# Attention and FFN in one kernel: when the rest rows' weights are combined, and how they are stored

## The chip, the cores and the metric

One of the 8 cores of a Trainium2 chip runs the whole kernel. The metric is the device time of one execution in microseconds (us). TensorE (PE) multiplies, VectorE (DVE), ScalarE (ACT) and GpSimd (POOL) work element by element, SyncE (SP) issues nearly all DMAs of this kernel. Each engine works its instructions off in program order.

## The reference

```python
def _A_ref(x, wqkv, wo):                       # B=1, S=2048, D=576
    H = 32; Dh = D // H; W, dil = 8, 2
    q, k, v = ...                              # x @ wqkv, per head
    idx = pos[:, None] - off[None, :]          # off = arange(W) * dil
    logits = einsum("bhsd,bhswd->bhsw", q, kg) * Dh ** -0.5   # masked where idx < 0
    attn = softmax(logits)
    return einsum("bhsw,bhswd->bhsd", attn, vg) ... @ wo
def _B_ref(x, w1, b1, w2):                     # F = 4608
    h = x @ w1 + b1
    act = h * tanh(softplus(h))                # Mish
    return act @ w2
xn = _layernorm(x)
return x + _A_ref(xn, A_wqkv, A_wo) + _B_ref(xn, B_w1, B_b1, B_w2)
```

Attention looks at 8 earlier tokens, two apart. All tensors are float32.

## The kernel before, in words

**Tiling.** The 2048 tokens are worked in two halves (hf 0 and 1) of 1024, each in two blocks of 512. Every float32 operand of a matmul is split into a high part (a cast to fp32r, ScalarE) and a low part (a subtraction, VectorE), and a product is three matmuls. QKV and the first FFN matmul (w1) are computed as a Strassen-like scheme of 7 products (B11, B21, B22, T3, T1, T2, T4) over 4 of the 4.5 tiles of 128 that make up D = 576. The sums of activations that it needs are S0 to S3 (`s_step`, GpSimd; `s_high`, ScalarE; `s_low`, VectorE). The last 64 rows of D, two blocks of 32, are the rest: their products, high and low rows side by side on the 128 partitions, need only one matmul for each of the 7 (`xt,wr`, `rest_y,xt` in the profile).

**Stages.** First layer norm, transposes and the first units of QKV (steps "q": PE lines 361, 363, 670, 676), which I call the prologue. Then QKV's second half by the 7 products (steps "y", line 791). Then 18 quads of the FFN for half 0, each of six parts of w1 (line 1100) with pairs of the w2 matmul (line 1197) between them, and attention's element work on GpSimd and VectorE underneath. Then the transition: QKV of half 1 (steps "v" and "z"), and the quads of half 1, which use what half 0 kept in DRAM (`kept_...`). The output projection comes last.

**Chunks.** The rest rows of the weights have to be combined (four subtractions give the other combinations from four blocks) and split as well. This is done for chunks: 0 to 3 (128 rows for four quads of w1 each), 4 (64 rows, two quads), and y and v (QKV). A chunk goes through five functions, one plan step apart: `c_load` (SyncE, line 869), `c_sum` (4 subtractions on GpSimd, line 874), `c_high` (cast on ScalarE, line 877), `c_low` (subtraction on VectorE, line 881) and `c_keep` (2 stores to the DRAM tiles `ckept`, line 889). Later `wr_fetch` (line 896) loads the 7 x 128 rest weights of a quad into one of the two buffers "wc", and `rest_fetch` (line 905) those of y, v and z. Before the change all seven chunks are made in the prologue. ck_4 has the buffer of ck_v and can be loaded when ck_v has been stored.

**What sets the order.** The program first makes a list `plan` of steps, each with foreground and background functions, filled by `put`, `before` and a table `MOVED`; then it runs the list, and each engine has its instructions in the order in which they were written. `spot(hf, q, i)` is slot i of quad q. A DMA that SyncE issues also waits for the one eight earlier on its lane, since there are eight semaphore lanes.

**Other names.** `rest_dup` copies the rest rows four times side by side before the transposes; `rest_split` splits what the transposes give; `qkv_send` stores finished rows of k, v and q in DRAM (`kv_d`, `q_d`, lines 691 and 696), from which attention reads them (lines 916 and 925).

## Time and profile before

| | |
|---|---|
| median of 3 runs | 1179.85 us (1179.37 to 1182.48) |
| profiled execution, its time | 1179.86 us |
| its span, first to last instruction | 1177.8 us |
| mean granted clock of TensorE | 0.971 |
| busy share PE, PEld, DVE, ACT, POOL | 93%, 85%, 77%, 45%, 68% |
| HBM read and written | 180.51 MB and 115.38 MB |

PEld is TensorE's weight load, which goes on beside the matmuls. In the rows of slices, the span is cut in 40 and a digit is the busy share in tenths; PEclk is the granted clock in tenths of full speed. A row of waits reads: engine and line that waited, the tile it needed, what made it last, then us in total, times, and the longest. In a row of the timeline the square bracket holds the idle time before it and what ended that. In a row of the chain stand start, us, engine or DMA and what it worked on.

### The profile page before, as it was taken

The page shows a single profiled execution, that of the slowest core. Times are in us where ns is not written, and L with a number is a line of the kernel's source. Part 1 is how long each engine was busy: PE and PEld are TensorE (multiplying, and loading weights), DVE is VectorE, ACT ScalarE, POOL GpSimd, SP SyncE. Part 2 cuts the span into 40 slices and gives each one's busy share as a digit, 9 for nine tenths or more (in the row PEclk, how much of TensorE's full clock was granted, in tenths as well). Part 3 has the DMA queues.
Part 4 walks back from the last instruction along what each step waited for, and adds up shares of the span by engine and source line. Part 5 has one row for each costly group of instructions (what it writes and reads, how often), then busy time and mean ns, then how long its engine had stood idle before and what let it go on. Part 6 is the DMA issues. An engine that isn't in the chain of part 4 may idle for free.

```text
span 1177.8 us, 18410 instructions
## 1 busy us (share of the span) xinstructions
PE 1094.1 (93%) x6414; PEld 999.1 (85%) x6414; DVE 911.9 (77%) x1505; ACT 525.0 (45%) x975; POOL 800.8 (68%) x649
## 2 busy tenths in 40 slices
PE   8706999999999999999988888999999999999998
PEld 7605989999999999989987767998988998999998
DVE  7608679888989878898786546688788888688886
ACT  7503555455445544445642205444443444244343
POOL 5207549767885777897587546977868688978533
PEclk9857999999999999999999989999999999999999
DMA  7545989988788787977479989988676867679864
GB/s 261 178 141 168 299 288 362 320 279 261 224 295 275 244 260 261 312 245 280 138 257 274 286 254 303 331 279 262 206 247 206 274 197 238 198 257 310 266 209 145
DMA packets 203300, 297.13 MB, mean 252 GB/s; under 512 B 63334, under 2 KB 137608, under 8 KB 203208
## 3 DMA queue, kind: packets, MB, share of 16 engines
q1 hardware_dynamic: 203208, 295.96, 77.9%
q8 instruction: 51, 0.84, 0.3%
q14 instruction: 41, 0.34, 0.1%
HBM read 180.51 MB, written 115.38 MB: 251 GB/s over the span
## 4 chain that ended last, share of the span: by engine, by line
PE 72%; DMA 10%; POOL 6%; DVE 5%; issue 3%; SPq 2%; ACT 2%; POOLq 0%; DVEq 0%; ACTq 0%
PE h L1100 29%; PE po L1197 16%; PE po L1289 10%; PE po L1311 6%; PE o L1476 5%; PE y L791 2%; POOL pv L1000 2%; DMA ckept_v<-ck_v 1%; DMA ckept<-ck 1%; DMA acc<-in_x 1%; POOL pr L961 1%; PE z L791 1%; DMA wr<-ckept 1%; DMA q<-q_d 1%; PE yT L791 1%
## 5 line engine op out<-in xcount | busy, mean ns | idle before, releaser
L1197 PEld LDWEIGHTS po<-w,act 128*128 128x128 f32 x1728 | 236.0, 188 | 7.7 <-DVE acc L1201 2.6
L1197 PE MATMUL po<-w,act 128*128 128x288 f32 x1728 | 241.1, 295 | 1.2 <-DVE acc L1201 1.1
L961 POOL TENSOR_TENSOR pr<-q,kv 128x576 f32<-128x576 f32 x128 | 194.3, 1544 | 26.0 <-DMA q<-q_d 11.8
L1000 POOL TENSOR_TENSOR pv<-L,kv 128x576 f32<-128x576 f32 x128 | 173.3, 1454 | 51.0 <-DVE L L993 13.6
L1150 POOL TENSOR_TENSOR act<-c,act 128x512 fp32r<-128x512 f32 x66 | 90.9, 1377 | 80.5 <-ACT act L1148 74.1
L1289 PEld LDWEIGHTS po<-pw,u 128*128 128x128 f32 x1008 | 137.8, 188 | 6.4 <-issue 2.0
L1289 PE MATMUL po<-pw,u 128*128 128x288 f32 x1008 | 141.1, 295 | 1.5 <-DMA pw<-kept_T 0.8
L1201 DVE TENSOR_TENSOR acc<-po,acc 128x288 f32<-128x288 f32 x288 | 118.8, 448 | 26.5 <-PE po L1197 25.1
L1006 DVE TENSOR_REDUCE og<-pv 128x144 f32<-128x1152 f32 x64 | 86.1, 1347 | 33.1 <-POOL pv L1000 33.1
L1100 PE MATMUL h<-xt,t 128*128 128x512 f32 x432 | 110.9, 391 | 0.7 <-DVE rt L1142 0.5
L1100 PE MATMUL h<-S,t 128*128 128x512 f32 x432 | 110.3, 391 | 0.0
L1100 PE MATMUL h<-xt,wa 128*128 128x512 f32 x432 | 109.8, 389 | 0.0
L1100 PE MATMUL h<-xt,wr 128*128 128x512 f32 x252 | 98.3, 390 | 3.7 <-DMA wr<-ckept 3.7
L1143 ACT ACTIVATE c<-c,cb 128x512 f32<-128x512 f32 x69 | 50.0, 725 | 108.9 <-DVE c L1142 108.8
L966 DVE TENSOR_REDUCE L<-pr 128x64 f32<-128x1152 f32 x64 | 85.5, 1340 | 16.6 <-POOL pr L961 16.4
L1100 PEld LDWEIGHTS h<-xt,wa 128*128 128x128 f32 x432 | 81.0, 188 | 16.5
L1100 PEld LDWEIGHTS h<-xt,t 128*128 128x128 f32 x432 | 78.9, 188 | 16.4 <-DVE rt L1142 1.3
L1100 PEld LDWEIGHTS h<-S,t 128*128 128x128 f32 x432 | 78.0, 188 | 13.2 <-ACT rm L1131 0.4
L670 PE MATMUL pq<-wq,xt 128*128 128x432 f32 x192 | 46.1, 387 | 38.9 <-ACT xt L367 38.0
L1311 PEld LDWEIGHTS po<-w,act 128*128 128x128 f32 x576 | 78.4, 188 | 1.6
L1311 PE MATMUL po<-w,act 128*128 128x288 f32 x576 | 79.5, 294 | 0.0
L1131 ACT COPY c<-h 128x512 f32<-128x512 f32 x68 | 39.8, 585 | 86.6 <-PE h L1100 86.6
(314 smaller groups left out, 2139.4 us busy)
## 6 DMA issues: line engine op xcount, KB each, us to landing
kv<-kv_d SPq DMA_DIRECT2D x64, 396.0 KB
kept_t<-t SPq DMA_DIRECT2D x36, 512.0 KB
t<-kept_t SPq DMA_DIRECT2D x36, 512.0 KB
wr<-ckept SPq DMA_DIRECT2D x72, 224.0 KB
pw<-kept_T SPq DMA_DIRECT2D x24, 576.0 KB
rw<-in_w SPq DMA_DIRECT2D x36, 288.0 KB
kept_B<-w SPq DMA_DIRECT2D x36, 288.0 KB
pw<-kept_B SPq DMA_DIRECT2D x18, 576.0 KB
```

The costliest lines, as they stand in the source:

```text
L961: nc.gpsimd.tensor_tensor(out=pr[:, x:x + hh], in0=q[:, j0 + x:j0 + x + hh, None, :].to_broadcast([P, hh, W, CU]), in1=win(kt, 0, CU, j0 + ...
L966: nc.vector.tensor_reduce(L[:, k, j0:j0 + hj].rearrange("p j w h -> p (j w h)"), pr.rearrange("p j w (h d) -> p (j w h) d", h=2), axis=AX, ...
L1000: nc.gpsimd.tensor_tensor(out=pr[:, x:x + hj].rearrange("p j d w -> p j w d"), in0=L[:, k, x:x + hj, :, h:h + 1].to_broadcast([P, hj, W, DH]),
L1006: nc.vector.tensor_reduce(og[:, c0:c0 + DH, :].rearrange("p d j -> p j d"), pr, axis=AX, op=ALU.add)
L1100: nc.tensor.matmul(ph, l, r_, start=first and i == 0, stop=i == len(seq) - 1, skip_group_check=True)
L1143: nc.scalar.activation(t, ph if fresh else t, AF.Mish, bias=b1c[:, f:f + 1])
L1150: eng.tensor_tensor(out=a[:, 1, :], in0=t, in1=a[:, 0, :].bitcast(F32), op=ALU.subtract)
L1197: nc.tensor.matmul(po, acts[hf, q, b, j][:, al, tok], done["w2", hf, 2 * q + j][:, wl, c * HC:(c + 1) * HC], start=i == 0, stop=i == 5)
L1201: nc.vector.tensor_tensor(out=t, in0=po, in1=t, op=ALU.add)
L1289: nc.tensor.matmul(po, units[e, k, qq][:, al, tok], w[:, qq, wl, :], start=i == 0, stop=i == 5)
L1311: nc.tensor.matmul(po, acts[hf, q, b, j][:, al, tok], done["w2", hf, 2 * q + j][:, wl, c * HC:(c + 1) * HC], start=i == 0, stop=i == 5)
L1476: nc.tensor.matmul(h, l, r_, start=first and n == 0, stop=n == len(seq) - 1, skip_group_check=True)
```

## The change

Only chunk 0 and y are made in the prologue. Chunks 1 to 4 and v are made as ten pieces of half the columns ("10", "11", ..., "41", "v0", "v1"), one in each of the quads 1 to 10 of half 0, in slots 0 (load), 1 (sum), 2 (high), 3 (low) and 4 (stores), in buffers of the tag "wc" that wr has too. wr of the next quad is fetched in slot 6 instead of 2 (q < 12). High and low rows alternate by partition instead of standing in blocks of 32; the DRAM tiles `ckept` have one row for each partition of a chunk, so that chunk 0 and y are stored as 128 rows. `qkv_send` of y, v and z comes a plan step later and in the background list. The last split of `rest_split` is a foreground function of the next step. In half 1 the sums S3 come ahead of S2.

On SyncE in the prologue (rows in program order; the shape behind the names is the access pattern), before, from the stores of ck_305 (chunk 2) on:

```order
L691 DMA kv_d_128<-kvs_0_1_446 128x8x144
L696 DMA q_d_132<-qs_0_1_447 128x4x144
L889 DMA ckept_627<-ck_305 4x32x896 x2
L723 DMA yB_0_633<-in_wq 128x432
L889 DMA ckept_v<-ck_v 4x32x756 x2
L869 DMA ck_4_659<-in_w1r 64x512
L723 DMA yB_0_662<-in_wq 128x432
L723 DMA yB_0_664<-in_wq 128x432
L889 DMA ckept_690<-ck_3_308 4x32x896
L889 DMA ckept_690<-ck_3_307 4x32x896
```

and now, from the stores of ck_301 (chunk 0) on:

```order
L895 DMA ckept_528<-ck_301 128x896 x2
L895 DMA ckept_y<-ck_y 128x756 x2
L596 DMA kept_wq_567<-wq_3_244 128x864
L723 DMA yB_0_569<-in_wq 128x432
L723 DMA yB_1_571<-in_wq 128x432
L691 DMA kv_d_128<-kvs_0_1_431 128x8x144
L696 DMA q_d_132<-qs_0_1_432 128x4x144
L723 DMA yB_0_594<-in_wq 128x432
L723 DMA yB_0_616<-in_wq 128x432
L723 DMA yB_0_618<-in_wq 128x432
L723 DMA yB_1_645<-in_wq 128x432
L723 DMA yB_1_668<-in_wq 128x432
```

The stores of chunks 1, 2, v and 3 and the load of ck_4 no longer stand between the loads of yB; the two chunks left have 128 rows in a store.

On ScalarE at the same place (xn_6 is the tile of tokens that is transposed next), before:

```order
L877 CAST ck_v<-ck_v 128x756
L331 CAST xt_1_569<-ss_0_585 128x4x128
L677 COPY kvs_0_1_446<-pq_0_1_3_608 128x8x36
L678 COPY qs_0_1_447<-pq_0_1_3_608 128x4x36
L877 CAST ck_3_308<-ck_3_307 128x896
L367 CAST xt_1_569<-ta_635 128x4x128
L331 CAST xt_1_569<-tb_636 128x128
L331 CAST a21t<-tb_636 128x128
L478 ACTIVATE xn_6_666<-acc_1_2_188,nm_167,rs_165 128x576
L380 COPY rd_6_668<-xn_6_666 128x256
```

and now:

```order
L677 COPY kvs_0_1_431<-pq_0_1_3_573 128x8x36
L678 COPY qs_0_1_432<-pq_0_1_3_573 128x4x36
L331 CAST xt_1_541<-ss_0_557 128x4x128
L367 CAST xt_1_541<-ta_596 128x4x128
L331 CAST xt_1_541<-tb_597 128x128
L331 CAST a21t<-tb_597 128x128
L478 ACTIVATE xn_6_620<-acc_1_2_188,nm_167,rs_165 128x576
L380 COPY rd_6_622<-xn_6_620 128x256
```

The casts of ck_v and ck_3 are gone, and the cast of xt from ss stands behind the copies of kvs and qs.

On ScalarE in quad 1 of half 0 (ck_1455 is the first piece, half of chunk 1), before:

```order
L1143 ACTIVATE c_0_1_1501<-c_0_1_1501,cb 128x512
L1148 CAST act_0_2_1523<-c_0_1_1501 128x512
L1131 COPY c_0_1_1555<-h_0_1_1493 128x512
L577 CAST w_0_3_1594<-rw_3_1464 128x576
L577 CAST t_0_2_1596<-tt_1514 128x512
L1131 COPY c_0_1_1608<-h_0_1_1493 128x512
L630 CAST twhT_1_1617<-twT_1_1559 128x576
```

and now:

```order
L1150 ACTIVATE c_0_1_1443<-c_0_1_1443,cb 128x512
L1155 CAST act_0_2_1467<-c_0_1_1443 128x512
L1138 COPY c_0_1_1500<-h_0_1_1435 128x512
L883 CAST ck_1455<-ck_1455 128x448
L577 CAST w_0_3_1540<-rw_3_1406 128x576
L577 CAST t_0_2_1542<-tt_1458 128x512
L1138 COPY c_0_1_1555<-h_0_1_1435 128x512
L630 CAST twhT_1_1567<-twT_1_1505 128x576
```

The cast of the piece stands ahead of the casts of w and t and of the second copy of c.

On SyncE in the same quad, before:

```order
L596 DMA kept_wc_1491<-wc_1_1442 128x512
L916 DMA kv_0_2_1541<-kv_d_127 128x792
L925 DMA q_2_1543<-q_d_131 128x288
L896 DMA wr_2_1545<-ckept_503 64x896 x2
L596 DMA kept_t_1_1598<-t_0_1_1462 128x1024
L596 DMA kept_wa_1612<-wa_2_1519 128x1024
L500 DMA rw_5_1614<-in_w 128x576
```

and now:

```order
L903 DMA wr_2_1614<-ckept_528 64x1x896 x2
L596 DMA kept_t_2_1631<-t_0_2_1542 128x1024
L500 DMA rw_4_1633<-in_w 128x576
L500 DMA rw_6_1635<-in_w 128x512
L500 DMA rw_7_1637<-in_w 128x512
L645 DMA kept_T_0_1639<-twhT_1_1567 256x1x288
L646 DMA kept_T_0_1639<-twT_1_1505 256x1x288
L592 DMA kept_B_0_1675<-w_0_2_1453 128x2x288
L592 DMA kept_B_0_1677<-w_0_3_1540 128x2x288 x2
L645 DMA kept_T_0_1683<-twhT_1_1612 256x1x288
L646 DMA kept_T_0_1683<-twT_1_1557 256x1x288
```

The load of the piece follows kept_wc; its two stores follow kept_t, and wr_2 comes behind them and behind kept_wa and rw_5.

On SyncE in the transition, before:

```order
L839 DMA z_B_0_0_6804<-kept_yB_0_941 128x432
L839 DMA z_B_0_1_6805<-kept_yB_0_941 128x432
L691 DMA kv_d_127<-kvs_v_6727 128x8x144
L696 DMA q_d_131<-qs_v_6726 128x4x144
L839 DMA z_B_1_0_6836<-kept_yB_1_968 128x432
L839 DMA z_B_1_1_6837<-kept_yB_1_968 128x432
L905 DMA rest_v_6847<-ckept_v 64x8x108 x2
L916 DMA kv_0_12_6879<-kv_d_130 128x792
```

and now:

```order
L839 DMA z_B_0_0_6847<-kept_yB_0_883 128x432
L839 DMA z_B_0_1_6848<-kept_yB_0_883 128x432
L839 DMA z_B_1_0_6876<-kept_yB_1_910 128x432
L839 DMA z_B_1_1_6877<-kept_yB_1_910 128x432
L912 DMA rest_v_6890<-ckept_v 64x4x216 x2
L691 DMA kv_d_127<-kvs_v_6769 128x8x144
L696 DMA q_d_131<-qs_v_6768 128x4x144
L923 DMA kv_0_12_6924<-kv_d_130 128x792
```

The stores of kvs_v and qs_v moved behind the loads of z_B and rest_v.

The diff, cut to these parts:

```diff
         last_ = []
-        plan[now[0] + 1][1].append(lambda: last_.append(split(X[:, 9:13, at_], ss)))
-        plan[now[0] + 2][1].insert(0, lambda: last_[0]())
+        plan[now[0] + 1][0].append(lambda: last_.append(split(X[:, 9:13, at_], ss)))
+        plan[now[0] + 1][0].append(lambda: last_[0]())
...
-        nc.scalar.copy(t.rearrange("p (k c d) -> p k c d", k=2, c=4), xns[hf, n][:, KT * P:D].rearrange(
-            "p (k d) -> p k d", k=2)[:, :, None, :].to_broadcast([P, 2, 4, RB]))
+        nc.scalar.copy(t.rearrange("p (k c d e) -> p k c d e", k=2, c=2, e=2), xns[hf, n][:, KT * P:D].rearrange(
+            "p (k d) -> p k d", k=2)[:, :, None, :, None].to_broadcast([P, 2, 2, RB, 2]))
...
         if half and jj == JB - 1 and (add_ or name == "B22"):
-            qkv_send(hf, g0 + g, b, kvs, qs)
+            plan[now[0] + 1][1].append(lambda: qkv_send(hf, g0 + g, b, kvs, qs))
...
-    CORDER = ("B11", "B21", "B22", "T3", "T1", "T2", "T4")
+    CORDER = ("B11", "B21", "B22", "T3", "T2", "T1", "T4")
     chunk, ckept, rcols = {}, {}, {}
 
+    def c_tiles(c):
+        return 7, QC if c[0] in "yv" else P, 64 if c[0] == "4" else P
+
     def c_load(c):
-        n, w, rows = (7, QC, P) if c in "yv" else (7, P, P if c != "4" else 64)
-        tag = {"0": "S0", "1": "S1", "2": "S2", "3": "wa", "4": "pr", "y": "kv", "v": "pr"}[c]
-        if tag[0] == "S":
-            t = sb.tile([P, 2, 2 * TB], F32, tag=tag, bufs=1, name=f"ck_{c}")
-            lo, hi = (t[0:rows, k, 0:n * w].rearrange("p (n w) -> p n w", n=n) for k in range(2))
+        n, w, rows = c_tiles(c)
+        cols = slice(0, w)
+        if c == "0":
+            t = sb.tile([P, 2, 2 * TB], F32, tag="S0", bufs=1, name="ck_0")
+            lo, hi = (t[:, k, 0:n * w].rearrange("p (n w) -> p n w", n=n) for k in range(2))
+        elif c == "y":
+            lo, hi = (sb.tile([P, n, w], F32, tag="kv", bufs=3, name=f"ck{k}_y") for k in range(2))
         else:
-            lo, hi = (sb.tile([P, n, w], F32, tag=f"wa{k}" if tag == "wa" else tag, bufs=dict(wa=1, pr=2, kv=3)[tag],
-                              name=f"ck{k}_{c}")[0:rows] for k in range(2))
-        chunk[c] = lo, hi.bitcast(F32R)
-        src = wqr["vy".index(c)] if c in "yv" else w1r[int(c) * P:int(c) * P + rows]
-        nc.sync.dma_start(lo[:, 0:4], src)
+            cols = slice(int(c[1]) * w // 2, (int(c[1]) + 1) * w // 2)
+            t = sb.tile([P, 2, n, w // 2], F32, tag="wc", bufs=2, name=f"ck_{c}")
+            lo, hi = t[0:rows, 0], t[0:rows, 1]
+        chunk[c] = lo, hi.bitcast(F32R), cols
+        src = wqr["vy".index(c[0])] if c[0] in "yv" else w1r[int(c[0]) * P:int(c[0]) * P + rows]
+        nc.sync.dma_start(lo[:, 0:4], src[:, :, cols])
 
     def c_sum(c):
         lo = chunk[c][0]
-        for o, a, b in ((4, 3, 0), (3, 2, 3), (5, 2, 4), (6, 1, 5)):
+        for o, a, b in ((5, 3, 0), (3, 2, 3), (4, 2, 5), (6, 1, 4)):
             nc.gpsimd.tensor_tensor(out=lo[:, o], in0=lo[:, a], in1=lo[:, b], op=ALU.subtract)
 
     def c_high(c):
         nc.scalar.copy(chunk[c][1], chunk[c][0])
 
     def c_low(c):
-        lo, hi = chunk[c]
+        lo, hi, _ = chunk[c]
         nc.vector.tensor_tensor(out=lo.bitcast(F32R), in0=lo, in1=hi.bitcast(F32), op=ALU.subtract)
 
     def c_keep(c):
-        lo, hi = chunk[c]
-        m = lo.shape[0] // RB
-        ckept[c] = dram.tile([2, RB, CP, 7 * QC] if c in "yv" else [m, 2, RB, 7 * P], F32, name=f"ckept_{c}")
+        lo, hi, cols = chunk[c]
+        n, w, rows = c_tiles(c)
+        if c[0] not in ckept:
+            ckept[c[0]] = dram.tile([2, rows, n, w], F32, name=f"ckept_{c[0]}")
         for h, t in ((0, hi.bitcast(F32)), (1, lo)):
-            d = ckept[c][h].rearrange("r k n -> k r n") if c in "yv" else ckept[c][:, h]
-            nc.sync.dma_start(d, t.rearrange("p n w -> p (n w)"))
+            nc.sync.dma_start(ckept[c[0]][h][:, :, cols], t)
 
     def wr_fetch(hf, q):
         w = Q1[q] if hf else q
         t = done["wr", hf, q] = sb.tile([P, 7, P], F32R, tag="wc", bufs=2, name=f"wr_{hf}_{q}")
-        src = ckept[str(w // CP)][w % CP].rearrange("h r n -> (h r) n")
+        r0 = w % CP * RB
+        src = ckept[str(w // CP)][:, r0:r0 + RB].rearrange("h r n w -> r h (n w)")
         for k in range(2):
             nc.sync.dma_start(t[k * 64:(k + 1) * 64].rearrange("p n w -> p (n w)").bitcast(F32), src)
 
     def rest_fetch(which, n):
         c = "y" if which in "yz" else "v"
-        ops_ = ((0, 1), (3, 5), (4, 6), (2,))[n]
+        ops_ = ((0, 1), (3, 4), (5, 6), (2,))[n]
         m = len(ops_)
         t = sb.tile([P, CP, m, QC], F32R, tag="wc" if n < 3 else "wd1", bufs=2 if n < 3 else 1, name=f"rest_{which}{n}")
-        src = ckept[c].rearrange("h r k (n w) -> (h r) k n w", w=QC)[:, :, ops_[0]:ops_[-1] + 1:max(ops_[-1] - ops_[0], 1)]
+        src = ckept[c][:, :, ops_[0]:ops_[-1] + 1].rearrange("h (k r) n w -> r h k (n w)", k=CP)
         for k in range(2):
-            nc.sync.dma_start(t[k * 64:(k + 1) * 64].bitcast(F32), src)
+            nc.sync.dma_start(t[k * 64:(k + 1) * 64].rearrange("p k m w -> p k (m w)").bitcast(F32), src)
         for k, o in enumerate(ops_):
             rcols[which, CORDER[o]] = t[:, :, k]
...
         for k, d in ((0, 0), (1, 1), (2, 2), (3, 4 - c)):
-            before(first + 1 + d, lambda c=c, k=k: s_step(1, c, k))
-            before(first + 2 + d, lambda c=c, k=k: s_high(1, c, k))
-            before(first + 2 + d, lambda c=c, k=k: s_low(1, c, k))
+            a = {(0, 2): (0, 3), (0, 3): None, (1, 2): (1, 3), (1, 3): (0, 2)}.get((c, k), (c, k))
+            for f, e in ((s_step, 1), (s_high, 2), (s_low, 2)):
+                before(first + e + d, (lambda: None) if a is None else lambda f=f, a=a: f(1, *a))
+    for f, e in ((s_step, 5), (s_high, 6), (s_low, 6)):
+        put(at["t", 1, 1, 3] + e, lambda f=f: f(1, 1, 2))
...
-    for c, load_, sum_ in (("0", 0, 2), ("1", 0, 3), ("2", 0, 5), ("3", 0, 7), ("y", 1, 4), ("v", 1, 6), ("4", 9, 11)):
-        put(load_, lambda c=c: c_load(c), 0)
-        put(sum_, lambda c=c: c_sum(c), 0)
-        put(sum_ + 1, lambda c=c: c_high(c), 0)
-        put(sum_ + 2, lambda c=c: c_low(c), 0)
-        put(sum_ + 3, lambda c=c: c_keep(c), 0)
+    chunks = [(c, (l, k, k + 1, k + 2, k + 3)) for c, l, k in (("0", 0, 3), ("y", 1, 4))]
+    for n, c in enumerate(("10", "11", "20", "21", "30", "31", "40", "41", "v0", "v1")):
+        chunks.append((c, [spot(0, n + 1, i) for i in range(5)]))
+    for c, slots in chunks:
+        for i, f in zip(slots, (c_load, c_sum, c_high, c_low, c_keep)):
+            put(i, lambda f=f, c=c: f(c), 0)
...
-        put(spot(0, q - 1, 2) if q > 1 else z0 + (8, 12)[q], lambda q=q: wr_fetch(0, q))
+        put(spot(0, q - 1, 6 if q < 12 else 2) if q > 1 else z0 + (8, 12)[q], lambda q=q: wr_fetch(0, q))
         put(spot(1, q - 1, 2) if q > 1 else v1 + (8, 12)[q], lambda q=q: wr_fetch(1, q))
...
-    wqdp = np.ascontiguousarray(np.tile(rests[0:2], (1, 1, 4, 1)).transpose(0, 2, 1, 3))
+    wqdp = np.ascontiguousarray(np.tile(np.repeat(rests[0:2], 2, axis=2), (1, 1, 2, 1)).transpose(0, 2, 1, 3))
...
-    sign = np.zeros((4, RB, 2), np.float32)
-    sign[0::2, :, 0], sign[1::2, :, 0], sign[1::2, :, 1] = -1.0, 1.0, 1.0
+    sign = np.zeros((2, RB, 2, 2), np.float32)
+    sign[:, :, 0, 0], sign[:, :, 1, 0], sign[:, :, 1, 1] = -1.0, 1.0, 1.0
```

More of the change, by code (lines that the diff above doesn't have):

```diff
@@ L1061, in s_step @@
             Ss[hf, k] = sb.tile([P, 4, TB], F32R, tag=f"S{k}", bufs=1, name=f"S{k}_{hf}")
-        t = stmp[k] = s_tmp(k) if k else s0[hf, c]
+        t = stmp[hf, c, "t", k] = s_tmp(k) if k else s0[hf, c]
         if k == 1:
-            gp(t, stmp[0], p["A11"][0], ALU.subtract)
+            gp(t, s0[hf, c], p["A11"][0], ALU.subtract)
             gp(t, t, p["A11"][1], ALU.subtract)
         elif k == 2:
-            gp(t, p["A12"][0], stmp[1], ALU.subtract)
+            gp(t, p["A12"][0], stmp[hf, c, "t", 1], ALU.subtract)
             gp(t, t, p["A12"][1], ALU.add)
```

## The prediction

> **What bounds the kernel now.** I read the slices of the page first, for where TensorE is idle, then stretches of 20 and 25 us, then the waits and the chain of work there.
>
> ```profile
> PE   8706999999999999999988888999999999999998
> PEclk9857999999999999999999989999999999999999
> DMA  7545989988788787977479989988676867679864
> q1 hardware_dynamic: 203208, 295.96, 77.9%
> ```
>
> A slice is 29.4 us. TensorE is idle in slice 3 and short in slice 2 and in slices 21 to 25; elsewhere it is the bound. DMA is no bound in slices 2 and 3 (4 to 5 tenths).
>
> ```profile
> 40.00:60.00 20.00, 10.96 (x48) 9.70 (x46) 10.93 (x20) 8.22 (x20) 6.17 (x10) 0.81 0.43 146
> 60.00:80.00 20.00, 0.00 (x0) 0.00 (x0) 0.00 (x0) 0.00 (x0) 0.00 (x0) 0.50 0.44 143
> 80.00:100.00 20.00, 6.39 (x25) 5.86 (x26) 6.28 (x9) 4.84 (x12) 6.30 (x8) 0.58 0.42 139
> 100.00:120.00 20.00, 13.98 (x61) 12.24 (x60) 19.93 (x17) 7.21 (x19) 15.75 (x11) 0.85 0.68 195
> ...
> PE pq L670 <- ACT xt L367: 38.0, 3, 36.9
> ...
> SPq L869 <- DMA ckept_v<-ck_v: 11.0, 1, 11.0
> ```
>
> Columns of the first four rows: stretch, its length, busy us of PE, PEld, DVE, ACT and POOL, granted clock, DMA share, GB/s. From 60 to 80 us no engine computes at all, and DMA runs at 0.44. TensorE waits 36.9 us at once for one cast of ScalarE. Who held that cast is in the chain and the timeline:
>
> ```profile
> 44.60 0.94 ACT ck L877
> ...
> 70.91 14.99 DMA ckept_v<-ck_v
> 85.97 4.16 DMA ck<-in_w1r
> ...
> 90.20 1.91 POOL L874 TENSOR_TENSOR ck<-ck 64x128 f32<-64x128 f32 x4 [37.06 <-DMA ck<-in_w1r]
> 93.61 4.12 PE L670 MATMUL pq<-wq,xt 128*128 128x432 f32 x12 [36.94 <-ACT xt L367]
> 95.97 1.26 DVE L881 TENSOR_TENSOR ck<-ck,ck 64x896 fp32r<-64x896 f32 x1
> 116.38 0.73 PE L791 MATMUL y<-yw_B,xt 128*128 128x432 f32 x1 [5.86 <-DVE yw_B L744]
> ```
>
> ck_4 can be loaded only when the store of ck_v has left its buffer (14.99 us for 378 KB), GpSimd sums it at 90.20, ScalarE casts it, and the cast of xt that TensorE needs is queued behind. From 93.59 VectorE has hardly a gap until 116.38 (19.93 of 20), when TensorE gets the weights of QKV's second half.
>
> Why is that store slow while DMA is at 0.4?
>
> ```profile
> q1 hardware_dynamic: 353, 1.18, 25.8%
> ```
>
> This is the queue between 44 and 56 us, when little but chunk stores is under way: 353 packets of about 3.3 KB use 25.8%, the share of 4 engines of 16. The stores of the old form (4x32x896) are served by a quarter of the engines, one after another, and what SyncE issues behind them queues up.
>
> The FFN of the first half:
>
> ```profile
> 155.00:180.00 25.00, 25.00 (x123) 21.18 (x122) 16.84 (x24) 17.51 (x31) 11.83 (x12) 1.00 1.03 344
> 180.00:205.00 25.00, 24.63 (x151) 22.18 (x150) 24.38 (x37) 12.75 (x22) 24.48 (x20) 1.00 1.01 364
> ...
> 280.00:305.00 25.00, 25.00 (x154) 22.97 (x154) 21.25 (x35) 12.53 (x21) 19.83 (x17) 1.00 0.80 256
> ```
>
> TensorE is full; a quad takes 23.85 us, read off the start of its part 0 from quad to quad. GpSimd has 5 us of slack a quad, DMA some 0.2 of it; but in the second row GpSimd and VectorE are full as well, and DMA is over 1 in the first two.
>
> **The change, part by part.** *Prologue.* Only chunk 0 and y stay in it, with stores of the form 128x896. Gone are the loads, 4 GpSimd sums, cast, subtraction and 2 stores each of chunks 1 to 4 and v, 10 stores in all.
>
> ```profile
> 41.36 0.39 ACT L677 COPY kvs<-pq 128x288 f32<-128x288 f32 x1
> ...
> 46.24 0.89 ACT L478 ACTIVATE xn<-acc,nm,rs 128x576 f32<-128x576 f32 x1
> 47.18 1.12 PE L361 MATMUL ta<-ident,xn 128*128 128x128 f32 x4 [5.71 <-ACT xn L478]
> 48.38 4.51 PE L670 MATMUL pq<-wq,xt 128*128 128x432 f32 x12
> ...
> 97.97 2.52 PE L670 MATMUL pq<-wq,xt 128*128 128x432 f32 x12
> ```
>
> The cast at 44.60 (it waited for the sums until 44.57) goes. The copies of kvs and qs and the moved cast of xt, now behind them, end at about 41.36 + 0.39 + 0.28 + 0.6, or 42.5; xn stood 0.79 us after the first cast of its item (45.45), so it starts at 43.3 and its transposes at 44.2 instead of 47.2: 3 us. The 12 matmuls behind took 4.51 us, where 2.52 is usual at full clock (the same twelve at 97.97), after an idle 5.71; with a shorter idle 2 us more come back. The next item, at 93.61 before, no longer waits for ck_4: it follows its predecessor, which ended at 56.7 and now ends at 51.7, so it stands near 52. That takes 41.6 us away. VectorE's run of 22.8 us to 116.38 loses the 1.26 of ck_4, and the restarted y matmuls lose some of their slow clock (22 in 6.24 us, later 28 in 5.5: about 2 us). 41.6 + 1.3 + 2 gives 45. Bounds: if the 22.8 us grows by a wait for yB or rest_y (rows of the prologue have 5 to 7 us for such a landing), 38; if VectorE's run, slowed beside GpSimd (1.7 us for an operation that took 0.9 alone), shortens too, 50.
>
> *Ten half chunks in quads 1 to 10.* A quad gets 1 load, 4 GpSimd subtractions of 128x64, 1 cast and 1 subtraction of 128x448, and 2 stores. From the rows: GpSimd at most 1.91 (four of 64x128), ScalarE 0.5 and VectorE 0.63 (half of 0.94 and 1.26). None is TensorE's; GpSimd's 5 us of slack cover them in most quads. Not in quad 1:
>
> ```profile
> 169.38 1.52 PE L1100 MATMUL h<-xt,wa 128*128 128x512 f32 x6
> ...
> 178.22 0.74 SPq L596 DMA_DIRECT2D kept_wc<-wc  x1
> ...
> 173.36 6.96 DMA rw<-in_w
> ...
> 182.06 2.99 POOL L1000 TENSOR_TENSOR pv<-L,kv 128x576 f32<-128x576 f32 x2
> ...
> 180.40 0.68 ACT L577 CAST w<-rw 128x576 fp32r<-128x576 f32 x1 [2.03 <-DMA rw<-in_w]
> ...
> 184.67 1.55 PE L1100 MATMUL h<-xt,t 128*128 128x512 f32 x6
> ```
>
> On SyncE's queue the load of the piece stands right behind kept_wc (178.22), 9 us into the quad that starts at 169.4, since SyncE is late there; with 6 to 7 us to land it is there near 185. GpSimd would sum at 182.06, so it waits 3 us and works 2. ScalarE's cast of the piece stands ahead of the cast of w that ran at 180.40 and of the copy of c behind it: they come at 187.5, 7 us later, and part 4 of the quad (184.67) needs the addition behind that copy: about 6 us of TensorE, and 2 for the slow clock behind such an idle. With 1 us spread over the rest: 9. Nothing, if the load lands earlier because the emptier prologue leaves SyncE less behind; 20, if quad 2, where SyncE is still 5 us late, pays as much and the others 0.5 each.
>
> wr, the rest weights of the next quad, is fetched four slots later, behind the piece's stores in SyncE's order, and waits for them to land (same buffer). In a quad starting at S the stores go at S + 11, land at S + 16 and wr lands at S + 22 to 23, needed at S + 25. Covered by some 3 us; without them TensorE would wait at every start of a quad (rival below).
>
> *Transition to the second half.*
>
> ```profile
> 605.79 1.42 SPq L839 DMA_DIRECT2D z_B<-kept_yB  x2
> 617.35 0.37 SPq L691 DMA_DIRECT2D kv_d<-kvs_v  x1
> ...
> PE zT L791 <- DMA rest_z<-ckept_y: 4.7, 1, 4.7
> PE z L791 <- DVE qs_z L796: 4.1, 1, 4.1
> PE vT L791 <- DMA rest_v<-ckept_v: 2.0, 1, 2.0
> PE v L791 <- DMA vw_B<-kept_wq: 2.0, 1, 2.0
> ...
> PE v L791 <- DVE S L1084: 1.1, 1, 1.1
> ```
>
> Before, SyncE's queue stands from 607.2 to 617.35 at the store of kvs_v, whose data VectorE has not made; behind it are z_B, rest_v, kv and q. The stores now come a step later, behind z_B and rest_v, so these need not wait: the 2.0 for rest_v and part of the 4.7 for rest_z go, and S3's sums, two GpSimd operations of 1.5 us earlier, end the wait for S (1.1). What is late next is attention of the second half, since kv of later rows is read from the stores moved back; GpSimd has gaps there. Of these rows' 13.9 us (with smaller ones some 18) I take 7 as gained; none, if the later kv costs what rest_v saves, 14 at most.
>
> *Rows alternating by partition* changes addresses and no count; rest_y, rest_v and rest_z now read two neighbouring combinations as 432 B instead of 2 x 216 B pieces, fewer packets, counted at nothing. In the prologue the QKV stores behind rest_y cost nothing either: their readers come 20 us later.
>
> Sum against the profiled execution (1179.86 us, span 1177.8; the median of the runs is 1179.85): 1179.9 - 45 + 9 - 7 = 1137.
>
> **The rivals.** *Small pieces.* The half chunks are moved in pieces of 256 B: 512 for a load and 896 for a store, 2304 a quad. What one costs is bounded by
>
> ```profile
> q1 hardware_dynamic: 1692, 0.38, 70.1%
> ```
>
> which is 651 to 654 us, nearly all small: 0.701 x 16 x 3 us / 1692 = 20 ns for 224 B on average; and by the whole span, 0.779 x 16 x 1177.8 / 203208 = 72 ns for 1456 B. 2304 pieces are 2.9 us of all 16 engines at 20 ns and 10.4 at 72. DMA has 0.2 x 23.85 = 4.8 us free in a quad. I take 20 ns, the row nearest in size, which fits. At 72 each quad becomes 5.6 us longer, the first two more: over 56 us, against gains of 52, and the kernel ends near 1193, slower. It decides from about 63 ns a piece. The Trainium skill, "DMA: Bandwidth & Descriptors", section "Specifications", gives 512 B as the smallest transfer for line rate, with a read-modify-write below it. By that rule the pieces of 256 B are the dear kind; the 20 ns for 224 B speak against a large price, though much of that window may be reads.
>
> *wr late in every quad.* If the pieces' stores land 5 to 7 us later than counted, the 3 us of cover are gone and each of ten quads waits 2 to 4: 1137 - 9 + 20 to 40 = 1148 to 1168. For it speak the DMA shares of 0.9 to 1.0 in quads 1 to 4; against it 0.75 to 0.8 later.
>
> *The idle 36.9 us is only half given back.* VectorE, GpSimd's S sums or the loads of yB take the place of the chunks: 1137 + 22 = 1159. Against it: VectorE and GpSimd are at 0.00 from 60 to 80 us, and the DMA share is 0.44.
>
> **How the numbers follow.** Forecast (1120 to 1147, the bounds of its three terms partly together): 0.66. wr late: 0.14. Half the idle: 0.10. Small pieces: 0.06, most of it slower. Something better than all this, or mixed: 0.04. The range of 1120 to 1160 leaves out the upper end of the second and third, and the fourth. Faster by over 0.3% (3.5 us, about what a measurement of this kernel tells from no change) 0.93, the same 0.02, slower 0.05.
>
> **What would show it.** Right: the stretch 60 to 80 us is full of TensorE, y starts near 71 to 73, no wait of TensorE over 6 us before it, and the chunk stores of the prologue land in 5 us or so. In quad 1 one wait of TensorE near part 4 for VectorE's c, of 4 to 8 us. In quads 3 to 10 TensorE at 24.5 of 25 or more, and few waits for wr; DMA share near 0.9. In the transition no stop of SyncE near 10 us at kv_d, and waits of some 11 instead of 18 us. Wrong: waits for wr at every start of a quad, a DMA share over 1 up to quad 10, or y starting near 95.

## The result: 1% faster, not 4%

| | median | range | runs |
|---|---|---|---|
| before | 1182.04 us | 1179.37 to 1183.5 | 5 |
| changed | 1169.44 us | 1168.16 to 1173.12 | 5 |

The ratio is 0.9904, 95% interval 0.988 to 0.9927. The profiled execution of the changed kernel took 1173.12 us with a span of 1171.3, against 1179.86 and 1177.8: 6.5 us between the spans. It has the longest time of its five runs and the one of before one of the shortest, so the profiles show about half of the 12.6 us between the medians. From the chunk functions on, lines of the changed kernel stand six or seven further down (w1's matmul is L1107, the pieces are at L875, L880, L883, L887 and L895).

Stretches of the changed kernel's profile, first the prologue, then three from the quads:

```profile
40.00:60.00 20.00, 18.32 (x97) 16.59 (x96) 16.12 (x26) 12.29 (x32) 10.39 (x11) 1.00 0.86 256
60.00:80.00 20.00, 13.47 (x56) 12.23 (x55) 19.97 (x18) 9.38 (x26) 15.30 (x11) 0.83 0.64 202
...
180.00:205.00 25.00, 21.03 (x118) 18.73 (x117) 17.69 (x29) 10.31 (x18) 18.10 (x19) 0.93 0.84 252
...
280.00:305.00 25.00, 23.12 (x141) 20.92 (x140) 21.71 (x33) 11.11 (x20) 18.94 (x19) 1.00 0.87 274
305.00:330.00 25.00, 22.91 (x138) 20.74 (x137) 19.51 (x33) 9.38 (x16) 17.01 (x15) 1.00 0.81 274
```

Most of the prologue's idle is filled; from 60 to 80 us VectorE is full now (19.97 of 20). The quads had 24.6 to 25 us of TensorE in 25 before. Now the three stretches shown have 21 to 23, and nothing else in them is full: VectorE has at most 21.71, GpSimd 18.94, DMA 0.87.

Where it went can be read from fixed points in TensorE's timeline: the y matmul behind the wait for its weights (five y matmuls stand ahead of that wait), and the first matmul on wr in quads 1 and 12 of half 0 and in quad 4 of half 1. Before (y at 116.38, shown above):

```profile
170.74 0.44 PE L1100 MATMUL h<-xt,wr 128*128 128x512 f32 x1
...
434.82 0.39 PE L1100 MATMUL h<-xt,wr 128*128 128x512 f32 x1
...
774.80 0.39 PE L1100 MATMUL h<-xt,wr 128*128 128x512 f32 x1
```

Changed:

```profile
71.40 0.73 PE L791 MATMUL y<-yw_B,xt 128*128 128x432 f32 x1 [6.53 <-DVE yw_B L744]
...
127.76 0.39 PE L1107 MATMUL h<-xt,wr 128*128 128x512 f32 x1
...
426.27 0.39 PE L1107 MATMUL h<-xt,wr 128*128 128x512 f32 x1
...
768.25 0.39 PE L1107 MATMUL h<-xt,wr 128*128 128x512 f32 x1
```

y goes on 116.38 - 71.40 = 45.0 us earlier. Two of these are lost behind it, where the granted clock is 0.91 from 100 to 120 us, and quad 1 is 43.0 us ahead; in the seven experiments with the same prologue it is 45.4 to 46.0. Quad 12 is 8.6 us ahead, so the eleven quads from 1 to 11 gave back 34.4; quad 4 of half 1 is 6.6 us ahead, so the transition gave back 2.0; from there little changes up to the end.

What TensorE waited for in the changed kernel from 100 to 600 us:

```profile
PE h L1107 <- DVE c L1149: 11.1, 4, 6.3
PE h L1107 <- ACT c L1138: 10.7, 6, 4.0
PE po L1204 <- POOL act L1157: 2.1, 1, 2.1
```

Before, the only wait for c there was one of 0.2 us. What stood behind it on ScalarE and SyncE (126 to 430 us; SyncE's row names the operation that ScalarE did last before):

```profile
ACT ck L883 <- POOL ck L880: 50.7, 8, 9.5
```

```profile
SPq L895 <- ACT t L577: 69.7, 9, 9.6
SPq L592 <- DVE w L578: 7.2, 3, 4.0
SPq L895 <- ACT w L577: 5.7, 1, 5.7
```

Quad 3 shows how one of these comes about (it starts at 183.1):

```profile
187.60 1.15 POOL L560 TENSOR_TENSOR tt<-rw,rw 128x256 f32<-128x256 f32 x1 [2.91 <-DMA rw<-in_w]
188.61 0.67 ACT L577 CAST w<-rw 128x576 fp32r<-128x576 f32 x1
192.38 3.33 POOL L968 TENSOR_TENSOR pr<-q,kv 128x576 f32<-128x576 f32 x2
195.68 1.26 POOL L1157 TENSOR_TENSOR act<-c,act 128x512 fp32r<-128x512 f32 x1
196.90 1.38 POOL L880 TENSOR_TENSOR ck<-ck 128x64 f32<-128x64 f32 x4
198.31 0.56 ACT L883 CAST ck<-ck 128x448 fp32r<-128x448 f32 x1 [9.04 <-POOL ck L880]
199.31 0.58 ACT L1138 COPY c<-h 128x512 f32<-128x512 f32 x1
199.94 2.93 PE L1107 MATMUL h<-S,t 128*128 128x512 f32 x6 [3.97 <-ACT c L1138]
...
198.91 1.25 SPq L895 DMA_DIRECT2D ckept<-ck  x2
200.93 0.72 SPq L500 DMA_DIRECT2D rw<-in_w  x1
```

GpSimd waits 2.91 us for rw and works without a gap from 187.60 on; it reaches the piece's sums only 14 us into the quad, behind attention's products. ScalarE has nothing to do for 9 us and stands at the piece's cast; the copy of c behind it, which frees the bank for TensorE, comes 4 us late, and then TensorE starts at the slow clock (2.93 us for six matmuls, 1.53 usual). SyncE stands at the stores from 192.1 to 198.9 with rw behind them.

### The profile page after: what moved, and what is told of

Its sections match the earlier page's. It is cut to its first block, busy times and chain, and to the rows that moved or that the text cites. A ratio compares the mean times of both kernels' runs of the same rounds, so it can differ in the third digit from the quotient of the medians.

```text
span 1171.3 us, 18440 instructions
## 1 busy us (share of the span) xinstructions
PE 1099.9 (94%) x6414; PEld 1001.6 (86%) x6414; DVE 910.5 (78%) x1510; ACT 524.4 (45%) x980; POOL 798.8 (68%) x669
## 4 chain that ended last, share of the span: by engine, by line
PE 60%; DVE 10%; POOL 10%; DMA 9%; issue 5%; SPq 2%; ACT 2%; POOLq 0%; DVEq 0%
PE h L1107 25%; PE po L1296 10%; PE po L1204 8%; PE po L1318 7%; PE o L1483 5%; POOL act L1157 3%; POOL pr L968 3%; PE y L791 2%; DMA wr<-ckept 2%; POOL tt L560 2%; DMA rw<-in_w 1%; DVE acc L1208 1%; DMA acc<-in_x 1%; POOL pv L1007 1%; DMA pw<-kept_T 1%
## 5 line engine op out<-in xcount | busy, mean ns | idle before, releaser
L1204 PEld LDWEIGHTS po<-w,act 128*128 128x128 f32 x1728 | 238.4, 189 | 10.7 <-DVE acc L1208 2.9
L968 POOL TENSOR_TENSOR pr<-q,kv 128x576 f32<-128x576 f32 x128 | 194.2, 1545 | 27.4 <-DMA q<-q_d 11.3
L1107 PE MATMUL h<-xt,t 128*128 128x512 f32 x432 | 113.2, 397 | 11.5 <-DVE c L1149 11.1
L1107 PE MATMUL h<-S,t 128*128 128x512 f32 x432 | 112.6, 396 | 10.7 <-ACT c L1138 10.7
L1107 PE MATMUL h<-xt,wa 128*128 128x512 f32 x432 | 112.2, 396 | 0.0
L1107 PE MATMUL h<-xt,wr 128*128 128x512 f32 x252 | 99.7, 395 | 7.4 <-DMA wr<-ckept 7.4
L1107 PEld LDWEIGHTS h<-xt,t 128*128 128x128 f32 x432 | 79.6, 190 | 28.7 <-DVE c L1149 13.2
L1107 PEld LDWEIGHTS h<-S,t 128*128 128x128 f32 x432 | 78.9, 190 | 25.9 <-ACT c L1138 12.1
L1107 PEld LDWEIGHTS h<-xt,wa 128*128 128x128 f32 x432 | 82.5, 191 | 17.0
L1302 DVE TENSOR_TENSOR accP<-po,accP 128x288 f32<-128x288 f32 x156 | 62.8, 446 | 7.7 <-PE po L1296 7.3
L1149 DVE TENSOR_TENSOR c<-h,c 128x512 f32<-128x512 f32 x69 | 46.9, 681 | 25.9 <-PE h L1107 20.9
```

The lines of the kernel that those rows point to most:

```text
L968: nc.gpsimd.tensor_tensor(out=pr[:, x:x + hh], in0=q[:, j0 + x:j0 + x + hh, None, :].to_broadcast([P, hh, W, CU]), in1=win(kt, 0, CU, j0 + ...
L1107: nc.tensor.matmul(ph, l, r_, start=first and i == 0, stop=i == len(seq) - 1, skip_group_check=True)
L1204: nc.tensor.matmul(po, acts[hf, q, b, j][:, al, tok], done["w2", hf, 2 * q + j][:, wl, c * HC:(c + 1) * HC], start=i == 0, stop=i == 5)
L1302: nc.vector.tensor_tensor(out=t, in0=po, in1=t, op=ALU.add)
```

## Experiments

Each ran beside the kernel before on one chip (its medians 1181 to 1183). Only those under "Parts left out" leave work out.

**All chunks in the prologue, new stores (e1).** The old schedule and buffers of the seven whole chunks in the changed kernel (chunk 0's sums at step 2 again, where the change has 3), wr back in slot 2. The new form of the stores and the other parts of the change stay:

```diff
-    for n, c in enumerate(("10", "11", "20", "21", "30", "31", "40", "41", "v0", "v1")):
-        chunks.append((c, [spot(0, n + 1, i) for i in range(5)]))
+    for c, load_, sum_ in (("0", 0, 2), ("1", 0, 3), ("2", 0, 5), ("3", 0, 7), ("y", 1, 4), ("v", 1, 6), ("4", 9, 11)):
...
```

> The changed kernel, but all seven chunks are made whole in the prologue as before, at the old steps and in the old buffers, with wr fetched in slot 2; their stores keep the new form of 128 rows. Theory A (the idle 60 to 80 us came from the form of the stores, and the 35 us lost in quads 1 to 11 come from the pieces made there): y starts some 5 to 10 us later than in the changed kernel (71.4), since VectorE and ScalarE have five more chunks, and the quads run at 23.85 us again: about 1145 us (1138 to 1152). Theory B (the prologue has no room for the chunks whatever their form): y starts near 95 or later, 1155 to 1165 us.

Measured: 1147.6 us, ratio 0.9706 (0.9684 to 0.9728), 22 us under the changed kernel. y goes on at 85.80, 14 us later than in the changed kernel, where I gave 5 to 10. But the quads lose nothing: quad 1 is 31 us ahead of before, quad 12 32. Theory A holds for time and quads; its ground, the form of the stores, is the next run's.

**The same with the old form of stores (e5).** The loads of the rest weights read the tiles' old layout accordingly (not shown):

```diff
-            ckept[c[0]] = dram.tile([2, rows, n, w], F32, name=f"ckept_{c[0]}")
+            ckept[c[0]] = dram.tile([RB, 2, CP, n * w] if c in "yv" else [rows // RB, 2, RB, n * w], F32, name=f"ckept_{c[0]}")
...
-            nc.sync.dma_start(ckept[c[0]][h][:, :, cols], t)
+            d = ckept[c][:, h].rearrange("r k n -> k r n") if c in "yv" else ckept[c][:, h]
+            nc.sync.dma_start(d, t.rearrange("p n w -> p (n w)"))
...
```

> e1 (all chunks in the prologue) with one edit: the chunks' DRAM tiles are laid out so that the stores have the old form again (4x32x896, 4x32x756, 2x32x896), while high and low rows still alternate by partition and all else is as in e1 (1147.6). Theory A (the form of the stores made the idle): ck_4 is loaded 15 instead of 5 us behind the store of ck_v, the idle near 60 to 80 us is back, and nearly all of e1's gain is gone: 1172 to 1183 us. Theory B (the gain of e1 has other grounds: the moved cast of rest_split, the order of QKV's stores, fewer packets of rest_y): 1147 to 1160 us.

Measured: 1178.65 us, ratio 0.9977 (0.9962 to 0.9991): 31 of e1's 34 to 35 us are gone. Its stretch from 60 to 80 us:

```profile
60.00:80.00 20.00, 0.00 (x0) 0.00 (x0) 0.00 (x0) 0.00 (x0) 0.00 (x0) 0.50 0.44 148
...
70.84 14.81 DMA ckept_v<-ck_v
```

In e1 the same 378 KB stand in the chain with

```profile
49.80 6.08 DMA ckept_v<-ck_v
```

So the idle came from the form of the stores. The Trainium skill, "DMA: Bandwidth & Descriptors", section "Why a DMA increments its semaphore by 16 and not by 1", says that a DMA is spread over the largest number of engines up to 16 that divides the slowest dimension of both access patterns. By that rule 4x32x756 gets four engines and 128x756 sixteen; the DMA share of 25.8% in the prediction's row and the fall from 14.81 to 6.08 us agree.

**The pieces' sums a slot earlier (e2)**, `(0, 0, 2, 3, 4)` instead of `range(5)`:

```diff
-        chunks.append((c, [spot(0, n + 1, i) for i in range(5)]))
+        chunks.append((c, [spot(0, n + 1, i) for i in (0, 0, 2, 3, 4)]))
```

> The changed kernel with one edit: the four sums of a piece are put in slot 0 instead of 1, which on GpSimd sets them ahead of the two pr products and one act product in every second quad, instead of behind them. Theory A (TensorE waits for copies of c that stand behind ScalarE's cast of the piece, which waits for GpSimd's late sums): the cast comes some 4 us earlier in about half of the ten quads, and 10 to 20 of the 35 us come back: 1150 to 1160 us. Theory B (late stores and wr, or the DMA's small pieces): unchanged within 3 us, 1169. In quad 1, where the load itself is late, no change by either.

Measured: 1162.08 us, ratio 0.9829 (0.9808 to 0.985): 7 us back, short of the 10 to 20. Quad 3 still loses 4.9 us (5.8 in the changed kernel), and quad 1 now 10.7 instead of 7.8, since GpSimd itself stands 11.57 us at the piece's load.

**The sums on VectorE (e3)**, with the slots 0, 3, 4, 4, 5:

```diff
-            nc.gpsimd.tensor_tensor(out=lo[:, o], in0=lo[:, a], in1=lo[:, b], op=ALU.subtract)
+            (nc.vector if len(c) == 2 else nc.gpsimd).tensor_tensor(
+                out=lo[:, o], in0=lo[:, a], in1=lo[:, b], op=ALU.subtract)
...
```

> The changed kernel with the pieces' sums on VectorE instead of GpSimd, in slots 0 load, 3 sum, 4 high and low, 5 stores, wr in 6. Theory A: GpSimd is out of the piece's path, the cast stands behind one more copy of c and finds its sums ready: 20 to 30 us come back, 1140 to 1150 us. Theory B: 1165 to 1172 us, with TensorE waiting for wr. If VectorE, at 85 to 90% in the quads, has no room for four more short operations: near 1160, with waits for acc or c of VectorE in the middle of a quad.

Measured: 1162.06 us, ratio 0.983 (0.9806 to 0.9854). Theory A missed; the time is what the third case gave. VectorE waits 5.55 us for the load in quad 1 and is then late with c (5.92 us of TensorE), and in the middle of later quads with acc.

**The cast late (e4)**: slots 0, 1, 6, 6, 7, wr in 8.

```diff
-        chunks.append((c, [spot(0, n + 1, i) for i in range(5)]))
+        chunks.append((c, [spot(0, n + 1, i) for i in (0, 1, 6, 6, 7)]))
-        put(spot(0, q - 1, 6 if q < 12 else 2) if q > 1 else z0 + (8, 12)[q], lambda q=q: wr_fetch(0, q))
+        put(spot(0, q - 1, 8 if q < 12 else 2) if q > 1 else z0 + (8, 12)[q], lambda q=q: wr_fetch(0, q))
```

> The changed kernel with the cast and the subtraction of a piece in slot 6 instead of 2 and 3, its stores in 7 instead of 4 and wr in 8 instead of 6. The cast then stands behind the last copy of c in the quad. Theory A: the waits of TensorE for c of ScalarE or VectorE in quads 1 to 10 go (some 25 us), but wr lands after the start of the next quad, 2 to 4 us each: 1160 to 1172 us, with TensorE's waits for wr at 20 us or more. Theory B (stores and wr bound the quads already now): each quad loses the 5 us that the stores come later, 1190 us or more.

Measured: 1201.68 us, ratio 1.017 (1.0136 to 1.0204). TensorE from 120 to 560 us:

```profile
PE h L1107 <- DMA wr<-ckept: 41.2, 10, 8.1
PE po L1204 <- DVE acc L1208: 8.6, 2, 7.8
```

The waits for c are gone, as A has it, but wr is 3 to 8 us late each time, and the time is the one that B gave: the cover of 3 us for wr, which I had counted, is used up by two slots and more. None of the four placings run so far suits both sides.

**Parts left out.** Four kernels split the 35 us; each omits one or more of the five functions for the ten pieces. Without the split (e9; likewise in `c_low`):

```diff
     def c_high(c):
-        nc.scalar.copy(chunk[c][1], chunk[c][0])
+        if len(c) == 1:
+            nc.scalar.copy(chunk[c][1], chunk[c][0])
...
```

> The changed kernel without ScalarE's cast and VectorE's subtraction of the ten pieces; the sums are stored twice in their stead, so the rest weights of quads 4 to 17 and of v are not split in this run. Loads, GpSimd's sums, the stores and wr's wait for them stay. Theory A (ScalarE's queue stands at the cast, which waits for GpSimd: 50.7 us of waits in the changed kernel, and the copies of c that TensorE needs are behind it): most of the 35 us of the quads come back, 1138 to 1148 us. Rival (SyncE's queue stands at the stores, 75 us of waits, and with it the loads of rw and wr): since the stores still wait for GpSimd, 1155 to 1165 us, and TensorE waits for c or wr late in the quads as before.

Without the stores (e10):

```diff
     def c_keep(c):
...
+        if len(c) == 2:
+            return
...
-        src = ckept[str(w // CP)][:, r0:r0 + RB].rearrange("h r n w -> r h (n w)")
+        src = ckept["0"][:, r0:r0 + RB].rearrange("h r n w -> r h (n w)")
...
```

> The changed kernel without the twenty stores of the pieces; wr of all quads is read from chunk 0's tile and rest_v from y's, so the results of quads 4 to 17 and of v are of wrong weights in this run. Loads, sums, cast and subtraction of the pieces stay. Theory A: ScalarE's wait for GpSimd is untouched, the loss stays at 20 to 35 us: 1155 to 1168 us. Rival (SyncE standing at the stores): it is gone, 1138 to 1148 us.

Measured: 1162.18 us without the split, 0.9841 (0.981 to 0.9872), and 1160.71 without the stores, 0.9824 (0.9803 to 0.9844). Each time lies in the range of the theory that blames the other queue, so neither holds alone: 7 and 9 us. Without the split SyncE still stands at the stores, 42.4 us for GpSimd, and GpSimd waits 19.0 us for rw; without the stores ScalarE still stands at the cast:

```profile
SPq L898 <- POOL ck L880: 42.4, 8, 9.3
```

```profile
ACT ck L883 <- POOL ck L880: 47.8, 8, 11.2
```

(the first of the kernel without the split, the second of that without stores). So two more, one with both edits (e12), and one that also leaves out the sums (e13):

```diff
     def c_sum(c):
         lo = chunk[c][0]
+        if len(c) == 2:
+            return
```

> The changed kernel with only the loads and GpSimd's sums of the ten pieces: no cast, no subtraction, no stores; the rest weights of quads 4 to 17 and of v are read from chunks 0 and y, so their results are of wrong weights in this run. Leaving out the split alone gave 1162.2, the stores alone 1160.7, some 8 of the 35 us each. If two queues stand independently (ScalarE at the cast, SyncE at the stores) and each alone delays the next operation of TensorE, both have to go: at least 25 us come back, 1132 to 1145 us. If the sums in GpSimd's order, with the products of attention and act behind them, are the ground of both: 1150 to 1160 us.

> The same, with the loads alone (no sums either). Neither queue nor GpSimd is held; what is left are the loads of 512 pieces of 256 B and wr fetched four slots later: 1130 to 1138 us, near the 1137 of my forecast less its 9 for the quads. If it is above 1145, the load, its wait for the buffer of wr on SyncE, or the late wr cost by themselves.

Measured: 1143.61 us with the sums alone, 0.9675 (0.9643 to 0.9706), and 1132.49 with the loads alone, 0.9579 (0.9545 to 0.9612). Split and stores together are worth 26 us, more than the 7 and 9 alone; the sums another 11. With the sums left, the quads still lose 12.9 us, 7.0 of them in quad 1, where GpSimd stands 5.59 us at the late load. With loads alone the quads run as before (w1's matmul is L1114 there):

```profile
125.26 0.39 PE L1114 MATMUL h<-xt,wr 128*128 128x512 f32 x1
...
389.42 0.39 PE L1114 MATMUL h<-xt,wr 128*128 128x512 f32 x1
```

264.16 us for eleven quads, 264.08 before. The loads of 256 B pieces and wr's later fetch cost nothing. Leaving out the stores also takes away their packets and wr's wait for them; no run separates these from SyncE's standing.

**The transition's parts.** In e1, QKV's stores sent at once (e7), and the old order of the sums (e8):

```diff
-            plan[now[0] + 1][1].append(lambda: qkv_send(hf, g0 + g, b, kvs, qs))
+            qkv_send(hf, g0 + g, b, kvs, qs)
...
```

> e1 with the stores of y's, v's and z's QKV rows sent at once as before the change, instead of a step later. By my prediction the later send frees SyncE for z_B, rest_v and rest_z, so that the wait of SyncE of 10 us at kv_d is back and 3 to 5 us are lost: 1150 to 1153 us. Rival: the waits of the transition are elsewhere (S for vT, qs_z, wr), and the time is the same within 1.5 us.

```diff
-            a = {(0, 2): (0, 3), (0, 3): None, (1, 2): (1, 3), (1, 3): (0, 2)}.get((c, k), (c, k))
...
+            before(first + 1 + d, lambda c=c, k=k: s_step(1, c, k))
...
```

> e1 with the S sums of the second half in the old order (S2 of the first 256 columns ahead of S3). By my prediction the new order saves two GpSimd operations on the way to S3: 2 to 3 us slower than e1, 1150 us. Rival: the new order only moves the wait to vT (5.0 us for S3's low part in e1, 2.0 us for rest_v before): then it is the same within 1.5 us, or up to 3 us faster than e1.

Measured: 1147.55 (0.9707, 0.9686 to 0.9728) and 1147.89 (0.9717, 0.9697 to 0.9736), both e1's 1147.6 within what can be told. With the stores sent at once SyncE stands 8.3 us at kv_d again, and the 3 to 5 us are not lost: my reason for that part falls. For the order of the sums the 2 to 3 us that I expected lie inside the two intervals (some 2.3 us each way), so that run settles nothing. The profiles hint at a gain that is lost again later: from quad 12 to the first quad of half 1, e1 and the eleven other profiles with all of the new transition gain 1.1 to 4.2 us on before, the one with the old order loses 0.8.

**Two numbers of e1's schedule (e6; e11 has 13 for the 15).**

```diff
-    for c, load_, sum_ in (("0", 0, 2), ("1", 0, 3), ("2", 0, 5), ("3", 0, 7), ("y", 1, 4), ("v", 1, 6), ("4", 9, 11)):
+    for c, load_, sum_ in (("0", 0, 2), ("1", 0, 3), ("2", 0, 5), ("3", 0, 6), ("y", 1, 4), ("v", 1, 6), ("4", 9, 15)):
```

> e1 with two numbers changed: the sums of chunk 3 at step 6 instead of 7 (with its cast, subtraction and stores), those of chunk 4 at step 15 instead of 11. In e1 TensorE still waits 5.8 us for xn (behind ScalarE's cast of chunk 3, which waits for GpSimd) and 6.0 us for xt (behind the cast of ck_4). Theory A: both waits go, with some slow clock behind them: 9 to 14 us less than e1, 1134 to 1139 us. Rival: VectorE's run of 20 us before y is the bound, and the later chunk 4 lengthens it by its subtraction and by GpSimd's four operations between the S sums: 0 to 4 us less, 1143 to 1148 us.

> e6 (1139.9 us) with the sums of chunk 4 at step 13 instead of 15. In e6 its four GpSimd operations and its subtraction of 2.1 us stand in the middle of the S sums and of VectorE's run to y (75.0), while VectorE waits 3.3 us for yB just before. At step 13 the subtraction falls into that wait: 1 to 4 us less than e6, 1136 to 1139 us. Rival: the S sums start 2.5 us later, and it is the same within 1 us or up to 2 slower.

Measured: 1139.85 us, ratio 0.9642 (0.9624 to 0.966), the best kernel here that does all the work, a little above theory A's 1134 to 1139. With step 13 for chunk 4 it is 1144.8, 0.9684 (0.9668 to 0.9701): 5 us more than at step 15, where the rival gave at most 2. Why so much was not followed up.

## Why the prediction was wrong, step by step

**Prologue: right, its exactness by luck.** 45 us were forecast, and y goes on 45.0 us earlier, at 71.40 in the span named. But the sum had 41.6 up to the matmuls that stood at 93.61 before, 1.3 for VectorE's run and 2 behind the start of y. The first came out larger:

```profile
49.69 2.74 PE L670 MATMUL pq<-wq,xt 128*128 128x432 f32 x12
```

That is 43.9 us, VectorE's run shrank by 1.1, and behind y nothing was gained in this profile (43.0 us at quad 1; 45.4 to 46.0 in the other seven). A wait of 6.53 us before y stayed, where I had named none over 6. The ground given was right, but less was needed: with the new form of the stores and all chunks still in the prologue, e1 is 31 us ahead at quad 1, and e5, with the old form, 1. The operation of VectorE that I gave 0.9 us alone takes 0.59 to 0.60 where it is not slowed; only the bound of 50 used it.

**The ten half chunks: the step that failed.** The sum had 9 us: 8 for quad 1 and 1 "spread over the rest". Quad 1 lost 7.8, by the mechanism described:

```profile
142.23 1.39 POOL L880 TENSOR_TENSOR ck<-ck 128x64 f32<-128x64 f32 x4 [4.18 <-DMA ck<-in_w1r]
143.65 0.56 ACT L883 CAST ck<-ck 128x448 fp32r<-128x448 f32 x1 [9.53 <-POOL ck L880]
147.49 2.93 PE L1107 MATMUL h<-xt,t 128*128 128x512 f32 x6 [6.32 <-DVE c L1149]
```

Quads 2 to 11 lost 26.6 instead of 1. "GpSimd's 5 us of slack cover them in most quads" weighed busy time against the quad's length. What counts is the moment at which each queue comes to the piece. I worked out that moment for quad 1 only, where a late load moves it, and took for the others that the load in time is enough. In quad 3 the load was in time, and the sums came at 14 us by GpSimd's own order. From there the same chain as in quad 1 ran: ScalarE's cast, the copy of c, TensorE. Over the ten quads with a piece, the later GpSimd comes to the sums, the more is lost, nearly without exception (us from the quad's start; loss against the same quad before):

| quad | 1 | 2 | 3 | 4 | 5 | 6 | 7 | 8 | 9 | 10 |
|---|---|---|---|---|---|---|---|---|---|---|
| sums at | 15.8 | 8.2 | 13.8 | 7.6 | 12.5 | 11.0 | 9.7 | 13.6 | 8.6 | 11.3 |
| loss | 7.8 | 0.0 | 5.8 | 0.4 | 3.3 | 2.7 | 0.7 | 5.1 | 1.4 | 2.8 |

From 7.6 to 9.7 us the quad bears it, with 1.4 us lost at most. The stores, which I had put at 11 us into every quad, go at 9.6 to 17.8. Quad 11, which has no piece, lost another 4.4; what of the pieces reaches into it was not followed up. The second thing that the sum lacked is SyncE: it stands at the pieces' stores for 75 us in all, with rw and kept_wa behind them. That is not 75 us more than before, since all its waits in these quads add up to 131 us now and were 124, mostly at other stores; what changed is which DMAs are late. e9, e10 and e12 show that each of the two queues alone keeps most of the loss.

**The rivals.** "wr late in every quad" gave 1148 to 1168 us, and the time lies just above its end, but that is chance, since the cause is another one: TensorE waited 0.9 us for wr in these quads, and only e4 makes wr late. Small pieces did not decide: with the loads alone nothing is lost, and while the two stores of quad 3 land (200 to 202 us) hardly any packets but those of 256 B are under way:

```profile
q1 hardware_dynamic: 1604, 0.41, 101.7%
```

That is 1.017 x 16 x 2 us / 1604 = 20 ns a packet, the 20 ns taken, well under the 63 from which it decides. The Trainium skill ("DMA: Bandwidth & Descriptors", "Specifications") gives 512 B as the smallest transfer for line rate. The trace agrees in that a byte is dearer in them: 256 B in 20 ns against 1456 B in 72 over the whole span before, over a third fewer bytes a second, which did not bind. The read-modify-write that the page names can't be seen here.

**Transition: wrong too.** 7 us were forecast as gained; these two profiles show 2 lost. In the eleven experiments with all of the new transition the same two points (quad 12, and quad 4 of half 1) lie between 2.8 lost and 2.9 gained against the one profile before. SyncE's stop at kv_d shrank from 10 to 4 us, and the waits for rest_v and most of that for rest_z are gone, but others grew:

```profile
PE z L791 <- DVE qs_z L796: 9.1, 1, 9.1
PE vT L791 <- DVE xt L1091: 5.0, 1, 5.0
...
PE zT L791 <- DMA rest_z<-ckept_y: 0.4, 1, 0.4
```

I took the waits in the rows as additive, and they are not. rest_z and qs_z together cost 8.8 us before and 9.5 now. What TensorE waits for at qs_z is held by attention, which the change did not speed up: before (first row) as now, GpSimd waits 8 us for q, VectorE stands at the sum over its products, and the addition to qs_z is queued behind.

```profile
683.74 5.58 POOL L961 TENSOR_TENSOR pr<-q,kv 128x576 f32<-128x576 f32 x4 [8.02 <-DMA q<-q_d]
...
672.73 5.48 POOL L968 TENSOR_TENSOR pr<-q,kv 128x576 f32<-128x576 f32 x4 [7.92 <-DMA q<-q_d]
675.52 1.35 DVE L973 TENSOR_REDUCE L<-pr 128x64 f32<-128x1152 f32 x1 [8.16 <-POOL pr L968]
681.59 2.53 PE L791 MATMUL z<-z_B,S 128*128 128x432 f32 x6 [9.14 <-DVE qs_z L796]
```

With rest_z there earlier, TensorE only reached this wait sooner. The same goes for vT: S3's subtraction is queued on VectorE behind attention's steps until 613.90. Which order would gain there stays open: e7 and e8 undo one part each and move no more than can be told, and both together and the moved cast of rest_split were not tried.

## What to carry to other kernels

Work put into a full loop must be placed in time on each queue that it passes, not weighed against that engine's slack: five short steps on four in-order queues cost 35 us here, though no engine was full. When one wait is removed and little comes back, remove its neighbours together: 7 and 9 us alone were 26 us as a pair. And before work is moved away from a stage, look at why the stage is slow: a store's outer dimension was worth 31 us with all chunks left where they were.

## What the runs showed of the hardware

Two stores of the same 378 KB, one with an outer dimension of 4 and one of 128, took 14.81 and 6.08 us, and in the profile before SyncE stood 11.0 us at the load that waits for the first. Packets of 256 B took 20 ns of one DMA engine each, where a mean packet, of 1456 B in the profile before, took 72. Behind the idles of TensorE of 3.97 and 6.32 us in quads 3 and 1 the first six matmuls took 2.93 us each time, for 1.53 usual, so such an idle cost at least 1.4 us more than its length. Between kernels with the same prologue quad 1 started at 124.8 to 127.8 us: the latest has a dip of the clock (0.91 between 100 and 120 us in the changed kernel's profile) that no wait explains.
